# Turning q and k by crossbar DMA transposes instead of on TensorE, in an attention plus feed-forward kernel

## The chip, the cores and the metric

One core of a Trainium2 chip. The time is the device time of one execution, in microseconds (us). Kernels that are compared were run in turn on the same chip. Runs of different sittings are set beside each other too; the kernel before took 235.2 to 236.7 us in all of them. In traces, PE is TensorE, PEld its weight loads, DVE is VectorE, ACT is ScalarE, POOL is GpSimd, SP is SyncE; a "q" after an engine is its queue of DMA issues. SBUF is the memory on the core; PSUM is the one into which TensorE writes.

## The reference, cut to what matters

```python
def _attn_ref(q, k, v, n_global, n_local):      # q, k, v: [4, 8, 768, 64]
    scores = scale * np.matmul(q, k.transpose(0, 1, 3, 2))
    # keep keys that are global (pos < 8) or at most 95 rows back; a bias by distance per head
    ...
    a = np.exp(scores - max); a = a / sum
    return np.matmul(a, v)

def _moe_ref(x, w_in, w_out):                   # x: [3072, 512], w_in: [512, 2048]
    h = np.maximum(x @ w_in, 0.0)
    return h * h @ w_out                        # ... cut
```

The attention output, [3072, 512], is the input of the feed-forward.

## The kernel before: the parts that matter

The 3072 rows are cut into eight half batches of 384 rows (numbered 0 to 7). While TensorE does the feed-forward of one half batch, the attention of the next is strewn among its matmuls. Two matmul layers take most of the time: "hps" (layer 1, 64 matmuls of 384 columns for each half batch) and "yps" (layer 2, 48 matmuls of 512 columns).

Scores need q and k with the head dimension on the partitions. The kernel before turns them on TensorE, and an engine that is free copies the result out of PSUM:

```python
def turn(x, a):                         # one pair of heads of half batch x
    def emit(e):
        state["ps"] = trp = ps_att.tile([P, 2, HT, P], FP16, name="trp", tag="att")
        for i, st in enumerate((x.sq, x.sk)):
            for t in range(HT):         # 2 x 3 transposes of 128x128
                nc.tensor.transpose(out=trp[:, i, t, :], in_=st[:, t, 2 * a:2 * a + 2, :],
                                    identity=ident)
    job = plan.pe(6 * 0.056, emit, x.q_in + x.k_in + [ident_op], [att])
    ...                                 # evac: PSUM to bt.qk, on ACT or DVE
    # fix_k: DVE copies parts of the turned k to bt.kb, the keys of the tile before
    x.qk_ops[a] = ops + [plan.add(costs, fix_k, [ops[1]])]
```

Two things decide the order of instructions. TensorE's own order is a list written by hand (`merge` puts attention jobs between feed-forward jobs). The order on DVE, ACT, POOL and SP comes from a planner that runs once, at build time: it gives each operation a cost and a time of landing, and always emits the one that could start first.

```python
class Plan:
    def load(self, dur, emit, needs=(), rank=None):
        op = Op({"POOL": 0.9}, emit, needs, rank, 1.0, land=dur)   # lag 1.0
    def run(self):
        while self.rest or any(self.queues.values()):
            ...                          # earliest possible start wins; ties go by rank
            op.done = end + op.lag       # when a later operation may count on it
            op.emit(e)                   # this fixes its place in the engine's queue
```

What the planner believes about time does not delay anything on the chip; there, semaphores do. But it decides which instruction stands in front of which, and each engine's queue keeps that order.

```python
y_p = ctx.enter_context(tc.tile_pool(name="yp", bufs=3))          # output rows
...
def evac(e):                             # in layer2
    y = y_p.tile([P, d_model], FP32, name="y", tag="y")
    copy(e, y, st["ps"])
    nc.sync.dma_start(out=out[r0:r0 + P, :], in_=y)               # SP's queue
```

q, k and v are loaded by POOL with a cast from float32 to float16, nine loads for each half batch.

The softmax here doesn't subtract the row's maximum and nothing guards it: scores larger than these inputs give would overflow.

Of the kernel before, what the change touches and what calls it, by code (L numbers as in the profile page):

```python
# [8 lines left out]
FP32 = mybir.dt.float32  # L9
# [4 lines left out]
P = 128  # L14
# [125 lines left out]
def kernel(  # L140
# [11 lines left out]
    nc = tc.nc  # L152
# [3 lines left out]
    d_model, d_ff = moe_w_in.shape  # L156
    NT = S // P
    NPAIR = H // 2
    NFT = d_ff // P
    NCT = d_model // P  # L160
    HALF = S // 2
    HT = HALF // P
    NHB = 2 * B
    GR = 32
# [16 lines left out]
    plan = Plan(1.0, 24.0)  # L181
# [5 lines left out]
    def copy(e, out, in_):  # L187
        if e == "ACT":
            nc.scalar.copy(out=out, in_=in_)  # L189
        else:  # L190
            eng(e).tensor_copy(out=out, in_=in_)  # L191
# [75 lines left out]
    def list_loads(x):  # L267
        r0 = x.half * HALF
        prev = halves[x.hb - 2] if x.hb >= 2 else None
        before = [prev.turned[-1]] if prev else []  # L270
        vbefore = [halves[x.hb - x.half - 3].attended[-1]] if x.hb >= 4 else []

        def rows(src, name, t):
            def emit(e):
                if getattr(x, name, None) is None and name != "v":
                    setattr(x, name, stage_p.tile([P, HT, H, D], FP16, name=name, tag=name))
                dst = (x.bt.v[:, x.half * HT + t, :, 0:D] if name == "v"
                       else getattr(x, name)[:, t, :, :])
                nc.gpsimd.dma_start(out=dst, in_=src[x.b, :, r0 + t * P:r0 + (t + 1) * P, :]  # L279
                                    .rearrange("h p d -> p h d"))  # L280
            return plan.load(0.62, emit, vbefore if name == "v" else before)

        if x.half == 0:
            def start(e):
                new_batch(x.bt)
                nc.vector.memset(x.bt.v[:, :, :, D:D + 1], 1.0)
            x.bt.op = plan.add({"DVE": 0.1}, start, vbefore, rank=0)
        if x.hb:
            x.q_in = [rows(q, "sq", t) for t in range(HT)]
            x.k_in = [rows(k, "sk", t) for t in range(HT)]  # L290
            x.v_in = [rows(v, "v", t) for t in range(HT)]
        else:
            raw = {n: stage_p.tile([P, HT, H, D], FP32, name=n, tag=n, bufs=1)
                   for n in ("rq", "rk")}
            x.q_in, x.k_in, x.v_in = [], [], []

            def fetch(name, src, t, eng, e, lag):
                op = plan.add({e: 0.5}, lambda e: eng.dma_start(
                    out=raw[name][:, t], in_=src[0, :, t * P:(t + 1) * P, :].rearrange(
                        "h p d -> p h d")), rank=-1)  # L300
                op.lag = lag
                return op

            def cast(dst, name, t, f):
                def emit(e):
                    if getattr(x, dst, None) is None:
                        setattr(x, dst, stage_p.tile([P, HT, H, D], FP16, name=dst, tag=dst))
                    copy(e, getattr(x, dst)[:, t], raw[name][:, t])
                return plan.add({"DVE": 0.42, "ACT": 0.54}, emit, [f], rank=0)
            k0 = fetch("rk", k, 0, nc.scalar, "ACT", 3.5)  # L310
            q0 = fetch("rq", q, 0, nc.sync, "SP", 3.5)
            x.q_in.append(cast("sq", "rq", 0, q0))
            x.k_in.append(cast("sk", "rk", 0, k0))
            for t in range(HT):
                if t:
                    x.q_in.append(rows(q, "sq", t))
                    x.k_in.append(cast("sk", "rk", t, fetch("rk", k, t, nc.sync, "SP", 4.0 + t)))
                if t < 2:
                    x.v_in.append(rows(v, "v", t))
            x.v_in.append(rows(v, "v", 2))  # L320
        for l in x.v_in:
            l.needs.append(x.bt.op)
# [15 lines left out]
    def tiles_before(x):  # L338
        return (1, HT - 1) if x.half == 0 else (HT - 1, NT - 1)

    def fix_v(x):
# [9 lines left out]
        costs = {"POOL": 0.6 + 2.1 * n} if x.hb > 1 else {"DVE": 0.2 + 0.65 * n}  # L351
        x.vb_op = plan.add(costs, emit, x.v_in)

    def turn(x, a):
        state = {}

        def emit(e):
            state["ps"] = trp = ps_att.tile([P, 2, HT, P], FP16, name="trp", tag="att")
            warm(trp.rearrange("p i t c -> p (i t c)"))
            for i, st in enumerate((x.sq, x.sk)):  # L360
                for t in range(HT):
# [4 lines that stand above are left out]
        def evac(i):  # L366
            def emit(e):
                copy(e, x.bt.qk[:, i, a, x.half * HALF:(x.half + 1) * HALF],
                     state["ps"][:, i].rearrange("p t c -> p (t c)"))
            return plan.after(job, {"ACT": 0.39, "DVE": 0.31}, emit)  # L370
        ops = [evac(0), evac(1)]
        t0, t1 = tiles_before(x)

        def fix_k(e):
            kt = x.bt.qk[:, 1, a, :].rearrange("p (t c) -> p t c", c=P)
            copy(e, x.bt.kb[:, a, t0 - 1:t1 - 1, GR:P], kt[:, t0:t1, GR:P])
            copy(e, x.bt.kb[:, a, t0 - 1:t1 - 1, 0:GR],
                 kt[:, 0:1, 0:GR].to_broadcast([P, t1 - t0, GR]))
        n = t1 - t0
        costs = {"DVE": 0.2 + 0.08 * n}  # L380
        if x.hb == 0:
            costs["POOL"] = 0.5 + 0.17 * n
        x.turned.append(job)
        x.qk_ops[a] = ops + [plan.add(costs, fix_k, [ops[1]])]

    GROUPS = {
        0: ([(0, 0), (1, 0), (1, 1)], [(2, 0), (2, 1)]),
# [161 lines left out]
    def layer2(x, j, m0):  # L549
        st = x.l2.setdefault(j, {})  # L550

        def emit(e):
            if m0 == 0:
                st["ps"] = ps_big.tile([P, 512], FP32, name="yps", tag="big")
            for m in range(m0, m0 + 4):
                nc.tensor.matmul(st["ps"], lhsT=x.h2[:, m, j * P:(j + 1) * P],  # L556
                                 rhs=w_out_sb[:, m, :], start=m == 0, stop=m == NFT - 1)
        job = plan.pe(4 * 0.216, emit, 
                      [x.h2_ops[max(c for c in x.h2_ops if c <= j * P)][m]
                       for m in range(m0, m0 + 4)] + [w_out_op[m0 // 4]], [big] if m0 == 0 else [])  # L560
        if m0 == 0:
            st["users"] = job.users
        else:
            job.users = st["users"]
            job.users[0].append(job)
        if m0 + 4 == NFT:
            def evac(e):
                y = y_p.tile([P, d_model], FP32, name="y", tag="y")
                copy(e, y, st["ps"])
                r0 = x.hb * HALF + j * P  # L570
                nc.sync.dma_start(out=out[r0:r0 + P, :], in_=y)
            plan.after(job, {"ACT": 0.52, "DVE": 0.63}, evac)

    for x in halves:
        x.turned, x.attended = [], []
# [97 lines left out]
    def tile_to_x(x, t, a0):  # L673
# [13 lines left out]
        for a in (a0, a0 + 1):  # L687
            x.x_ops[a, t] = op

    def attention(x):  # L690
        jobs = [lambda: fix_v(x)]
        for a in range(NPAIR + 3):
            if a < NPAIR:
                jobs.append(lambda a=a: turn(x, a))
            if 0 <= a - 1 < NPAIR:
                jobs.append(lambda a=a - 1: score(x, a))
            if 0 <= a - 2 < NPAIR:
                jobs.append(lambda a=a - 2: attend(x, a))
            if 0 <= a - 3 < NPAIR:
                jobs.append(lambda a=a - 3: to_x(x, a))  # L700
        return jobs

    def merge(main, side, start, stop):
        done = 0
        for i, f in enumerate(main):
            if i >= start:
                want = len(side) if i >= stop else (i - start) * len(side) // (stop - start)
                while done < want:
                    side[done]()
                    done += 1  # L710
            f()
        for f in side[done:]:
            f()

    def l1(x, m0=0):
        return [lambda m=m: layer1(x, [m]) for m in range(m0, NFT)]

    def l2(x):
        return [lambda j=j, m0=m0: layer2(x, j, m0) for j in range(HT) for m0 in range(0, NFT, 4)]
# [38 lines left out]
    for hb in range(1, NHB):  # L758
        x = halves[hb]
        if hb + 1 < NHB:  # L760
            list_loads(halves[hb + 1])
        main = l2(x0)[6:] + l2(x) if hb == 1 else l1(x) + l2(x)
        side = attention(halves[hb + 1]) if hb + 1 < NHB else []
        merge(main, side, 1, len(main) - 3)
    with tc.manual_schedule():
        order = plan.run()

# [34 lines left out]
```

## Time and profile before

The kernel before takes 235.71 us (median of 4 runs, 235.53 to 236.65). The page of its profile says, in this order: the span; busy time of each engine; busy tenths in 40 slices of the span, with the granted TensorE clock (the share of full speed at which the chip let TensorE run) in tenths and the DMA engines' share; the chain of waits that ended last; and two groups of DMA issues with the median time from issue to landing as their last number.

```profile
span 233.5 us, 5024 instructions
PE 221.1 (95%) x2023; PEld 133.8 (57%) x2023; DVE 126.0 (54%) x340; ACT 139.1 (60%) x319; POOL 86.2 (37%) x100
...
PE   7675999999999999999999999999999999999993
...
PEclk9999799999999999999999999999999999999999
DMA  8999999999159907951099107941002100111012
...
PE 88%; POOL 5%; DMA 4%; DVE 0%; issue 0%; ACT 0%; POOLq 0%
...
out_dram<-y SPq DMA_DIRECT2D x24, 256.0 KB, 2.0
...
sq<-in_q_dram POOLq DMA_DIRECT2D x23, 128.0 KB, 5.8
```

TensorE is busy for 90% or more of every slice from the fifth to the last but one, and the chain of waits is 88% TensorE. The waits of the other engines cost nothing there. The DMA row is full for the first ten slices (weights and first loads) and then comes and goes.

| | TensorE in one half batch, steady state |
|---|---|
| layer 1, layer 2 | 64 x 0.1625 + 48 x 0.216 = 20.8 us |
| scores, values, output turns | 4 x 0.45 + 4 x 0.34 + 4 x 0.17 = 3.8 us |
| q and k turns | 4 x 0.33 = 1.3 us |
| measured, start of layer 1 to the next start | 25.95 and 26.4 us in turn |

The turn is read from the timeline of TensorE (start, length, engine and line, what, how many):

```profile
106.62 0.33 PE L362 MATMUL trp<-ident,sq 128*128 128x128 f16 x3
106.78 0.33 PE L362 MATMUL trp<-ident,sk 128*128 128x128 f16 x3
106.95 1.46 PE L508 MATMUL hps<-xt,w_in_sb 128*128 128x384 f16 x8
```

From the first transpose to the next layer 1 matmul are 106.95 - 106.62 = 0.33 us for six transposes, 55 ns each. The length of the record (0.33 us for three) overlaps with the next; the spacing is what a turn costs. The Trainium skill, "TensorE: Matmul & The Clock Gate", Part 4, gives about 275 ns for one transpose in a kernel; in a row, this trace has 55 ns from start to start.

### The profile page before, as it was taken

What the parts mean: (1) busy time and instruction counts of PE and PEld (TensorE: products, weight loads), DVE (VectorE), ACT (ScalarE), POOL (GpSimd) and SP (SyncE); (2) the same over time, 40 slices, a digit from 0 to 9 for tenths busy, and PEclk for the clock granted to TensorE, in tenths of its full rate; (3) what the DMA queues carried; (4) which work ended last, traced back from release to release, by engine and by line L of the source; (5) the groups of instructions that cost most, each with busy time, mean ns of one, the idle gap of its engine ahead of it and who ended that gap; (6) DMA issues with size and microseconds to landing.
All of it is one profiled execution on the core that took longest, in us unless ns stands there. A gap on an engine that the chain in (4) does not pass through costs nothing.

```text
span 233.5 us, 5024 instructions
## 1 busy us (share of the span) xinstructions
PE 221.1 (95%) x2023; PEld 133.8 (57%) x2023; DVE 126.0 (54%) x340; ACT 139.1 (60%) x319; POOL 86.2 (37%) x100
## 2 busy tenths in 40 slices
PE   7675999999999999999999999999999999999993
PEld 6553689654555566556655565556655565556541
DVE  5395799441376279425864279325863279323300
ACT  4693797671564598328961598328961598327521
POOL 8948723894457307670292107560000000000000
PEclk9999799999999999999999999999999999999999
DMA  8999999999159907951099107941002100111012
GB/s 149 168 194 155 200 206 193 156 149 108 45 77 164 148 0 50 162 87 46 0 120 171 49 3 51 162 82 45 3 1 93 45 4 0 48 45 45 0 48 90
DMA packets 82583, 20.77 MB, mean 89 GB/s; under 512 B 75392, under 2 KB 79488, under 8 KB 82560
## 3 DMA queue, kind: packets, MB, share of 16 engines
q0 software_dynamic: 74944, 13.11, 74.5%
q1 hardware_dynamic: 6576, 7.08, 9.1%
q10 hardware_dynamic: 1040, 0.26, 0.5%
q8 instruction: 16, 0.26, 0.5%
q14 instruction: 7, 0.06, 0.1%
HBM read 27.26 MB, written 6.29 MB: 144 GB/s over the span
## 4 chain that ended last, share of the span: by engine, by line
PE 88%; POOL 5%; DMA 4%; DVE 0%; issue 0%; ACT 0%; POOLq 0%
PE hps L508 37%; PE yps L556 36%; PE sp L409 5%; PE trp L362 4%; DMA sk<-in_k_dram 4%; PE av L464 4%; PE trx L488 2%; POOL sq L279 2%; POOL v L279 1%; POOL sk L279 1%; POOL w_in_sb L327 1%; ACT y L189 0%; DVE ident L226 0%; DVE qk L191 0%; POOL dist L220 0%
## 5 line engine op out<-in xcount | busy, mean ns | idle before, releaser
L508 PE MATMUL hps<-xt,w_in_sb 128*128 128x384 f16 (+2 forms) x576 | 93.8, 311 | 0.2 <-DMA w_in_sb<-in_moe_w_in_dram 0.2
L556 PE MATMUL yps<-w_out_sb,h 128*128 128x512 f16 x384 | 91.9, 379 | 0.0
L508 PEld LDWEIGHTS <-w_in_sb 128*128 128x128 f16 x576 | 51.4, 99 | 27.7 <-DMA w_in_sb<-in_moe_w_in_dram 0.4
L532 ACT ACTIVATE hr<-hps 128x384 f16<-128x384 f32 (+1 forms) x109 | 56.3, 517 | 12.0 <-PE hps L508 9.8
L543 DVE TENSOR_TENSOR h<-hr 128x768 f16<-128x768 f16 (+1 forms) x68 | 36.8, 541 | 38.0 <-ACT hr L532 36.9
L556 PEld LDWEIGHTS <-h 128*128 128x128 f16 x384 | 34.5, 98 | 33.6
L424 ACT ACTIVATE ex<-sp 128x384 f16<-128x384 f32 x112 | 44.4, 510 | 4.2 <-PE sp L409 4.1
L189 ACT COPY y<-yps 128x512 f32<-128x512 f32 x22 | 12.9, 585 | 55.1 <-PE yps L556 55.1
L279 POOL DMA_DIRECT2D sq<-in_q_dram x23 | 20.8, 914 | 38.0 <-PE trp L362 36.5
L189 ACT COPY qk<-trp 128x384 f16<-128x384 f16 (+1 forms) x43 | 19.9, 506 | 11.4 <-DVE qk L191 10.4
L191 POOL COPY vb<-v 32x520 f16<-32x520 f16 (+3 forms) x18 | 19.3, 1070 | 19.1 <-DMA v<-in_v_dram 18.5
L279 POOL DMA_DIRECT2D v<-in_v_dram x24 | 21.4, 918 | 7.3 <-DMA w_out_sb<-in_moe_w_out_dram 3.3
L279 POOL DMA_DIRECT2D sk<-in_k_dram x21 | 18.6, 908 | 5.9 <-DMA w_out_sb<-in_moe_w_out_dram 3.1
L440 DVE TENSOR_TENSOR phat<-ex,mask 128x768 f16<-128x768 f16 x32 | 16.4, 553 | 5.4 <-ACT ex L424 5.1
L191 DVE COPY qk<-trp 128x384 f16<-128x384 f16 (+1 forms) x19 | 6.9, 365 | 17.5 <-PE trp L362 13.4
L473 DVE TENSOR_TENSOR tm<-av,rec 128x384 f16<-128x384 f32 x28 | 15.6, 557 | 1.0
L464 PEld LDWEIGHTS <-phat 128*128 128x128 f16 x312 | 13.2, 98 | 4.8
L464 PE MATMUL av<-v,phat 128*128 128x65 f16 x192 | 13.2, 193 | 0.0
L436 DVE TENSOR_TENSOR phat<-ex,mask 128x768 f16<-128x768 f16 (+1 forms) x24 | 10.7, 486 | 3.6 <-ACT ex L424 3.5
L464 PE MATMUL av<-vb,phat 128*128 128x65 f16 x120 | 12.1, 193 | 0.0
L191 DVE COPY kb<-qk 128x96 f16<-128x96 f16 (+4 forms) x58 | 10.2, 222 | 3.5 <-ACT qk L189 2.0
L362 PE MATMUL trp<-ident,sk 128*128 128x128 f16 x84 | 10.0, 226 | 1.5 <-DMA sk<-in_k_dram 1.5
(59 smaller groups left out, 154.8 us busy)
## 6 DMA issues: line engine op xcount, KB each, us to landing
out_dram<-y SPq DMA_DIRECT2D x24, 256.0 KB, 2.0
v<-in_v_dram POOLq DMA_DIRECT2D x24, 128.0 KB, 6.3
sq<-in_q_dram POOLq DMA_DIRECT2D x23, 128.0 KB, 5.8
sk<-in_k_dram POOLq DMA_DIRECT2D x21, 128.0 KB, 5.9
w_in_sb<-in_moe_w_in_dram POOLq DMA_DIRECT2D x4, 512.0 KB, 9.0
w_out_sb<-in_moe_w_out_dram POOLq DMA_DIRECT2D x4, 512.0 KB, 14.3
rk<-in_k_dram SPq DMA_DIRECT2D x2, 256.0 KB, 6.2
rk<-in_k_dram ACTq DMA_DIRECT2D x1, 256.0 KB, 4.6
```

What stands on the lines that cost most here:

```text
L189: nc.scalar.copy(out=out, in_=in_)
L191: eng(e).tensor_copy(out=out, in_=in_)
L279: nc.gpsimd.dma_start(out=dst, in_=src[x.b, :, r0 + t * P:r0 + (t + 1) * P, :] .rearrange("h p d -> p h d"))
L362: nc.tensor.transpose(out=trp[:, i, t, :], in_=st[:, t, 2 * a:2 * a + 2, :], identity=ident)
L424: nc.scalar.activation(out=st["ex", g][:, h, 0:n], in_=st[g][h][:, 0:n], func=AF.Exp, scale=scale)
L440: eng(e).tensor_tensor(out=phat[:, :, c0:c0 + n].rearrange("p e (i c) -> p e i c", c=P), in0=ex[:, :, 0:n].rearrange("p e (i c) -> p e i c ...
L464: nc.tensor.matmul(av[:, h, j, :], lhsT=phat[:, h, c * P:(c + 1) * P], rhs=rhs, start=n == 0, stop=n == len(mine) - 1)
L473: nc.vector.tensor_tensor(out=st["tm"].rearrange("p t e d -> p e t d"), in0=av[:, :, :, 0:D], in1=rec[:, :, :, None].to_broadcast([P, 2, H ...
L508: nc.tensor.matmul(st["ps"][:, i * n:(i + 1) * n], lhsT=w_in_sb[:, kk, m * P:(m + 1) * P], rhs=x.xt[:, kk, c0:c1], start=kk == 0, stop=kk ...
L532: nc.scalar.activation(out=o, in_=i, func=AF.Relu)
L543: eng(e).tensor_tensor(out=x.h2[:, m0:m0 + width, c0:c1], in0=hr, in1=hr, op=ALU.mult)
L556: nc.tensor.matmul(st["ps"], lhsT=x.h2[:, m, j * P:(j + 1) * P], rhs=w_out_sb[:, m, :], start=m == 0, stop=m == NFT - 1)
```

## The change

The turns of half batches 2 to 7 go from TensorE to the DMA engines. Six crossbar transposes (DMAs that transpose on their way) of 128 KB for each half batch, issued from SP's queue, write q and k turned straight into SBUF; no PSUM, no copy out. As TensorE is what bounds the kernel, 24 turns fewer should be 24 turns of time. The freed places are used to spread scores, values and output turns evenly over the feed-forward. Stores of the output become operations of their own in the plan, because they share SP's queue with the transposes.

```diff
-        before = [prev.turned[-1]] if prev else []
+        before = prev.turned if prev else []          # a load waits for these transposes
 ...
+    def turn_by_dma(x):
+        for t in range(HT):
+            for i, (src, loads) in enumerate((("sq", x.q_in), ("sk", x.k_in))):
+                def emit(e, i=i, t=t, name=src):
+                    nc.sync.dma_start_transpose(
+                        out=x.bt.qk[:, i, :, r0 + t * P:r0 + (t + 1) * P],
+                        in_=getattr(x, name)[:, t].rearrange("p h d -> p (h d)"))
+                op = plan.add({"SP": 1.2}, emit, [loads[t], x.bt.op])
+                op.lag = 2.5
+                ops.append(op)
+        x.turned += ops
+        for a in range(NPAIR):
+            x.qk_ops[a] = ops + [plan.add(*fix_k(x, a), ops)]     # kb copies, on DVE
 ...
-                nc.sync.dma_start(out=out[r0:r0 + P, :], in_=y)
+            plan.add({"SP": 0.6}, lambda e: nc.sync.dma_start(out=..., in_=st["y"]), [y_op])
 ...
     def attention(x):
+            jobs.append((0.02 + 0.2 * a, lambda a=a: score(x, a)))
+            jobs.append((0.02 + 0.2 * a + 0.17, lambda a=a: attend(x, a)))
+            jobs.append((0.02 + 0.2 * a + 0.3, lambda a=a: to_x(x, a)))
 ...
+            fix_v(halves[hb + 1])
+            turn_by_dma(halves[hb + 1])
-        merge(main, side, 1, len(main) - 3)
+        merge(main, side)
```

Cut: how `merge` places a job at its fraction of the feed-forward, and the removed TensorE branch.

More of the change, by code (lines that the diff above doesn't have):

```diff
@@ L352, in fix_v, with fix_k, emit @@
         x.vb_op = plan.add(costs, emit, x.v_in)
+    def fix_k(x, a):
+        t0, t1 = tiles_before(x)
+        def emit(e):
+            kt = x.bt.qk[:, 1, a, :].rearrange("p (t c) -> p t c", c=P)
+            copy(e, x.bt.kb[:, a, t0 - 1:t1 - 1, GR:P], kt[:, t0:t1, GR:P])
+            copy(e, x.bt.kb[:, a, t0 - 1:t1 - 1, 0:GR],
+                 kt[:, 0:1, 0:GR].to_broadcast([P, t1 - t0, GR]))
+        return {"DVE": 0.2 + 0.08 * (t1 - t0)}, emit
     def turn(x, a):
@@ L371, in turn @@
         ops = [evac(0), evac(1)]
-        t0, t1 = tiles_before(x)
-        def fix_k(e):
-            kt = x.bt.qk[:, 1, a, :].rearrange("p (t c) -> p t c", c=P)
-            copy(e, x.bt.kb[:, a, t0 - 1:t1 - 1, GR:P], kt[:, t0:t1, GR:P])
-            copy(e, x.bt.kb[:, a, t0 - 1:t1 - 1, 0:GR],
-                 kt[:, 0:1, 0:GR].to_broadcast([P, t1 - t0, GR]))
-        n = t1 - t0
-        costs = {"DVE": 0.2 + 0.08 * n}
-        if x.hb == 0:
-            costs["POOL"] = 0.5 + 0.17 * n
-        x.turned.append(job)
-        x.qk_ops[a] = ops + [plan.add(costs, fix_k, [ops[1]])]
+        x.turned.append(job)
+        x.qk_ops[a] = ops + [plan.add(*fix_k(x, a), [ops[1]])]
+    def turn_by_dma(x):
+        r0 = x.half * HALF
+        ops = []
+        for t in range(HT):
[10 more added lines that the diff above has]
+            x.qk_ops[a] = ops + [plan.add(*fix_k(x, a), ops)]
     GROUPS = {
@@ L567, in evac @@
             def evac(e):
-                y = y_p.tile([P, d_model], FP32, name="y", tag="y")
-                copy(e, y, st["ps"])
-                r0 = x.hb * HALF + j * P
-                nc.sync.dma_start(out=out[r0:r0 + P, :], in_=y)
-            plan.after(job, {"ACT": 0.52, "DVE": 0.63}, evac)
+                st["y"] = y_p.tile([P, d_model], FP32, name="y", tag="y")
+                copy(e, st["y"], st["ps"])
+            r0 = x.hb * HALF + j * P
+            y_op = plan.after(job, {"ACT": 0.52, "DVE": 0.63}, evac)
+            plan.add({"SP": 0.6}, lambda e: nc.sync.dma_start(out=out[r0:r0 + P, :], in_=st["y"]),
+                     [y_op])
     for x in halves:
@@ L690, in attention, with merge @@
     def attention(x):
-        jobs = [lambda: fix_v(x)]
-        for a in range(NPAIR + 3):
-            if a < NPAIR:
-                jobs.append(lambda a=a: turn(x, a))
-            if 0 <= a - 1 < NPAIR:
-                jobs.append(lambda a=a - 1: score(x, a))
-            if 0 <= a - 2 < NPAIR:
-                jobs.append(lambda a=a - 2: attend(x, a))
-            if 0 <= a - 3 < NPAIR:
-                jobs.append(lambda a=a - 3: to_x(x, a))
-        return jobs
-    def merge(main, side, start, stop):
-        done = 0
-        for i, f in enumerate(main):
-            if i >= start:
-                want = len(side) if i >= stop else (i - start) * len(side) // (stop - start)
-                while done < want:
-                    side[done]()
-                    done += 1
-            f()
-        for f in side[done:]:
-            f()
+        jobs = []
+        for a in range(NPAIR):
+            jobs.append((0.02 + 0.2 * a, lambda a=a: score(x, a)))
+            jobs.append((0.02 + 0.2 * a + 0.17, lambda a=a: attend(x, a)))
+            jobs.append((0.02 + 0.2 * a + 0.3, lambda a=a: to_x(x, a)))
+        return sorted(jobs, key=lambda j: j[0])
+    def merge(main, side):
+        for i, f in enumerate(main):
+            while side and side[0][0] * len(main) <= i:
+                side.pop(0)[1]()
+            f()
+        for _, g in side:
+            g()
     def l1(x, m0=0):
```

## The prediction

> **What bounds the kernel now.** TensorE. The busy table gives PE 95% of 233.5 us (221.1 us), ACT 60%, DVE 54%, POOL 37%. In the table by stretches PE is 20.00 of 20 us busy from 50 us to 210 us, and the chain of waits is 88% PE. The waits list gives PE only about 9 us of waits, all in the opening. So from about 52 us on the time is a sum of PE work. The timeline of PE shows one half batch in 25.95 us (104.02 to 129.97) or 26.42 us (77.60 to 104.02): feed-forward 64 x 0.1625 + 48 x 0.216 = 20.8 us, scores about 4 x 0.45, values 4 x 0.34, output turns 4 x 0.17, and the q/k turns 4 x 0.33 us (106.62 to 106.95 is one turn: six transposes 55 ns apart, though each record lasts 0.22 us).
>
> **What the change does.**
> - Removes from PE 24 turns (144 transposes) of half batches 2 to 7: 24 x 0.33 = 7.9 us, all on the critical path. Removes 48 PSUM-to-SBUF copies, 35 on ACT (0.50 us), 13 on DVE (0.36 us): shorter queues, no direct gain.
> - Adds 36 crossbar transposes of 128 KB on SP's queue, six per half batch, in 26 us. The Trainium skill ("Advanced Engine Details and Errata", X-Bar Transpose) calls them as fast as regular DMAs, 350-400 GB/s; that would be (estimate) 0.35 us of data each. No trace here shows one yet. With issue and completion (a plain 256 KB store lands in 2.0 us) I expect 1 to 2 us of queue each and 2 to 3 us to landing: under half the queue's time.
> - Moves scores and values. PE has less work between a score and its values: for pair 1, 16 layer-1 matmuls and a turn, 2.8 us plus the score's own 0.44. In half batches of odd number the trace shows exponentials 0.6 us after the score's start, 1.65 us long, then two mask products of 1.0 us: about 3.4 us. So I expect a small new PE wait, up to 0.5 us, there.
> - kb copies now wait for DMA and stand in DVE's in-order queue before mask products. If loads (about 4 us from last issue to landing) plus transposes are late, DVE blocks and PE follows. I work out half batch 5 as the tightest: its last k lands near 81.5 us, transposed near 84 us, and DVE gets there near 82.5 us; the mask product needs it only about 84.3 us. About 1 us of PE wait; half batches 4, 6 and 7 have a microsecond or so of room.
> - y stores stand behind transposes on SP; three y buffers cover about 10 us, enough.
>
> **Sum.** 235.6 - 7.9 + about 1.8 of new waits = 229.5 us. Opening and tail unchanged.
>
> **What would show it.** PE busy falls by about 8 us or a little more in busy time of records; a steady half batch takes 24.7 to 25.2 us; no turn of lines with "trp" after 32 us; transposes land in under 3 us; ACT busy falls by about 17 us; the waits list has PE values behind DVE mask products of under 3 us in all; DVE kb waiting for DMA of 1 to 4 us.
>
> **What would make it wrong.** Transposes that take over 3 us of queue each: kb late, DVE blocked, PE waiting several us per half batch, up to a loss. Less likely, y stores stuck behind them and PSUM held. On the good side, no new waits at all: 227.5 us.
>
> Faster by over 2% (under 230.9) 0.62, within 2% 0.31, slower 0.07.

## The result, and the profile after

The changed kernel takes 252.95 us (median of 4 runs, 251.23 to 253.35). The ratio to the kernel before is 1.0709, with a 95% interval of 1.0651 to 1.0766: 7% slower. Here and below a ratio is the mean time of one kernel's runs over that of the other's of the same rounds, so it is not quite the ratio of the medians quoted. Executions over 1.5% slower than the fastest of the same kernel are left out of the means.

```profile
span 250.9 us, 4778 instructions
PE 220.0 (88%) x1879; PEld 127.6 (51%) x1879; DVE 124.6 (50%) x322; ACT 127.2 (51%) x289; POOL 86.2 (34%) x100
...
PE   6764999997099498899997499999999999999994
...
PEclk9999799999779889999999779999999999999999
DMA  9999999999999999908999411002100210021012
...
PE 48%; DMA 35%; DVE 6%; POOL 5%; SPq 3%; issue 2%; ACT 0%; POOLq 0%; DVEq 0%
...
out_dram<-y SPq DMA_DIRECT2D x24, 256.0 KB, 2.0
...
sq<-in_q_dram POOLq DMA_DIRECT2D x23, 128.0 KB, 10.4
...
qk<-sq SPq DMA_TRANSPOSE x18, 7.2
```

TensorE's row now has holes in the slices from the tenth to the twenty-third, its share falls from 95% to 88%, and the granted clock dips to 0.7 or 0.8 beside the holes. The chain of waits is no longer TensorE's: 35% of it is DMA. The DMA row stays full up to the seventeenth slice. A transpose lands 7.2 us after its issue; the planner counted on 2.5 us. Loads of q land after 10.4 us instead of 5.8.

Where in time the loss arises shows in the start of layer 1 of each half batch, read from the timelines (us):

| | layer 2 begins | hb 2 | hb 3 | hb 4 | hb 5 | hb 6 | hb 7 | end |
|---|---|---|---|---|---|---|---|---|
| before | 51.67 | 77.60 | 104.02 | 129.97 | 156.39 | 182.34 | 208.75 | 233.5 |
| after | 51.87 | 91.07 | 118.44 | 151.14 | 176.50 | 201.12 | 226.48 | 250.9 |
| difference | 0.2 | 13.5 | 14.4 | 21.2 | 20.1 | 18.8 | 17.7 | 17.4 |

There are two kernels in one here. From 151 us on a half batch takes 25.36 or 24.61 us, 1.1 to 1.3 us less than before: the 0.33 us of each of the four turns are really gone. Before that, 21 us are lost. The list of waits (engine, line, what it waited for: us in all, times, longest) names the place:

```profile
DVE kb L191 <- DMA qk<-sk: 25.2, 4, 8.9
...
PE av L480 <- DVE phat L452: 11.3, 2, 7.9
...
PE trx L504 <- DVE tm L489: 5.1, 1, 5.1
...
PE av L480 <- DVE phat L456: 1.8, 3, 0.9
```

DVE stood for 25.2 us at copies to "kb" that wait for a transpose of k, four times. TensorE then waited 11.3 + 5.1 + 1.8 = 18.2 us for DVE. The timeline of DVE shows three of the four (the idle time before an instruction, and what ended it, in brackets):

```profile
66.30 2.36 DVE L191 COPY kb<-qk 128x288 f16<-128x288 f16 x6 [8.91 <-DMA qk<-sk]
68.58 0.87 DVE L452 TENSOR_TENSOR phat<-ex,mask 128x768 f16<-128x768 f16 x2
...
85.52 0.37 DVE L191 COPY kb<-qk 128x96 f16<-128x96 f16 x2 [5.60 <-DMA qk<-sk]
...
85.97 0.89 DVE L452 TENSOR_TENSOR phat<-ex,mask 128x768 f16<-128x768 f16 x2
...
139.63 1.28 DVE L191 COPY kb<-qk 128x288 f16<-128x288 f16 x2 [7.09 <-DMA qk<-sk]
140.84 0.17 DVE L487 RECIPROCAL rec<-av 128x6 f32<-128x6 f32 x1
```

DVE idled 8.9 us before the kb copies of half batch 3, 5.6 us before those of half batch 4 and 7.1 us before those of half batch 7. What stands behind them in the queue is of quite another half batch. At 139.63 us DVE waits for keys of half batch 7, whose scores TensorE computes from 201 us on; the reciprocal behind it, at 140.84 us, belongs to half batch 4 and is what TensorE needs now. The instruction listing of the built program shows the same order:

```
194 L559 TensorTensor h_1761<-hr 128x768 [waits Activation_49]
195 L191 TensorCopy kb<-qk 128x3x96 [waits DMAHW7_49,DMAHW6_49,DMAHW2_49]
196 L191 TensorCopy kb<-qk 128x3x32
197 L487 Reciprocal rec<-av 128x6 [waits PE_49]
```

TensorE's own timeline answers at the same moments:

```profile
69.17 0.57 PE L480 MATMUL av<-v,phat 128*128 128x65 f16 x4 [7.91 <-DVE phat L452]
...
70.65 2.70 PE L572 MATMUL yps<-w_out_sb,h 128*128 128x512 f16 x8
...
73.36 1.89 PE L572 MATMUL yps<-w_out_sb,h 128*128 128x512 f16 x8
...
86.57 0.57 PE L480 MATMUL av<-v,phat 128*128 128x65 f16 x4 [3.36 <-DVE phat L452]
```

It waited 7.9 us for the mask product at 68.58 us and 3.4 us for the one at 85.97 us. After the first wait eight layer 2 matmuls take 2.70 us; the next eight take 1.89 us. After this wait the granted clock was 0.62 (69.2 to 73.3 us), then 1.00 again (73.36 to 75.2 us); after the other two long waits it was 0.74 (86.6 to 92.0 us) and 0.50 (141.7 to 147.0 us).

The sum: between 51.87 and 151.14 us the changed kernel took 99.3 us, the one before 78.3 us, so 21.0 us more, although 12 turns (12 x 0.33 = 4.0 us) were gone. That makes 25 us of new loss, of which 18.2 us are the waits for DVE. The other 7 us fit the lower clock (0.83 from 57 to 77 us, 0.93 from 77 to 151 us): TensorE was busy for 81.1 of the 99.3 us at a mean clock of 0.91, and 0.91 x 81.1 = 73.8 us, while the kernel before without its 12 turns needs 78.3 - 4.0 = 74.3 us at full clock. No experiment separates the lower clock from the waits that come with it.

### The profile page after: what moved, and what is told of

Its sections match the earlier page's. It is cut to its first block, busy times and chain, and to the rows that moved or that the text cites. A ratio compares the mean times of both kernels' runs of the same rounds, so it can differ in the third digit from the quotient of the medians.

```text
span 250.9 us, 4778 instructions
## 1 busy us (share of the span) xinstructions
PE 220.0 (88%) x1879; PEld 127.6 (51%) x1879; DVE 124.6 (50%) x322; ACT 127.2 (51%) x289; POOL 86.2 (34%) x100
## 4 chain that ended last, share of the span: by engine, by line
PE 48%; DMA 35%; DVE 6%; POOL 5%; SPq 3%; issue 2%; ACT 0%; POOLq 0%; DVEq 0%
PE yps L572 24%; PE hps L524 17%; DMA v<-in_v_dram 15%; DMA w_out_sb<-in_moe_w_out_dram 6%; DMA qk<-sk 5%; DMA w_in_sb<-in_moe_w_in_dram 3%; DMA sk<-in_k_dram 3%; PE av L480 3%; PE sp L425 3%; SPq L392 2%; POOL vb L191 2%; DVE phat L456 2%; DVE h L559 2%; POOL v L279 2%; DMA sq<-in_q_dram 2%
## 5 line engine op out<-in xcount | busy, mean ns | idle before, releaser
L572 PE MATMUL yps<-w_out_sb,h 128*128 128x512 f16 x384 | 94.1, 393 | 0.0
L548 ACT ACTIVATE hr<-hps 128x384 f16<-128x384 f32 (+1 forms) x109 | 55.8, 512 | 20.3 <-PE hps L524 17.7
L572 PEld LDWEIGHTS <-h 128*128 128x128 f16 x384 | 36.5, 101 | 40.3 <-issue 5.3
L440 ACT ACTIVATE ex<-sp 128x384 f16<-128x384 f32 x112 | 43.8, 486 | 25.5 <-PE sp L425 25.5
L559 DVE TENSOR_TENSOR h<-hr 128x768 f16<-128x768 f16 (+1 forms) x68 | 38.0, 560 | 20.3 <-ACT hr L548 19.6
L191 DVE COPY kb<-qk 128x96 f16<-128x96 f16 (+4 forms) x58 | 12.9, 323 | 25.8 <-DMA qk<-sk 25.2
L480 PE MATMUL av<-v,phat 128*128 128x65 f16 x192 | 14.9, 200 | 11.9 <-DVE phat L452 11.3
L480 PEld LDWEIGHTS <-phat 128*128 128x128 f16 x312 | 13.6, 101 | 20.2 <-DVE phat L452 12.4
L456 DVE TENSOR_TENSOR phat<-ex,mask 128x768 f16<-128x768 f16 x32 | 17.7, 593 | 5.1 <-ACT ex L440 5.1
L550 DVE TENSOR_SCALAR hr<-hps 128x384 f16<-128x384 f32 x15 | 8.3, 556 | 17.8 <-PE hps L524 17.3
L191 DVE COPY xt<-trx 128x384 f16<-128x384 f16 (+1 forms) x18 | 6.2, 351 | 16.6 <-PE trx L504 16.6
L504 PE MATMUL trx<-ident,tm 128*128 128x128 f16 x84 | 9.3, 223 | 5.1 <-DVE tm L489 5.1
L487 DVE RECIPROCAL rec<-av 128x6 f32<-128x6 f32 x28 | 5.5, 197 | 14.6 <-PE av L480 13.7
## 6 DMA issues: line engine op xcount, KB each, us to landing
sq<-in_q_dram POOLq DMA_DIRECT2D x23, 128.0 KB, 10.4
```

The lines of the kernel that those rows point to most:

```text
L191: eng(e).tensor_copy(out=out, in_=in_)
L440: nc.scalar.activation(out=st["ex", g][:, h, 0:n], in_=st[g][h][:, 0:n], func=AF.Exp, scale=scale)
L456: eng(e).tensor_tensor(out=phat[:, :, c0:c0 + n].rearrange("p e (i c) -> p e i c", c=P), in0=ex[:, :, 0:n].rearrange("p e (i c) -> p e i c ...
L480: nc.tensor.matmul(av[:, h, j, :], lhsT=phat[:, h, c * P:(c + 1) * P], rhs=rhs, start=n == 0, stop=n == len(mine) - 1)
L504: nc.tensor.transpose(out=st["trx"][:, t, :], in_=st["tm"][:, t, :, :], identity=ident)
L548: nc.scalar.activation(out=o, in_=i, func=AF.Relu)
```

## The experiments

The theories:

- **A, placement.** The data come early enough. The planner put the kb copies where it believed a transpose has landed. DVE keeps that order, so it stands at a copy that nobody needs yet.
- **B, supply.** Loads and transposes together cannot bring q and k in time, wherever the copies stand.
- **C, order.** The even spread of scores and values on TensorE is what stalls.

And for the long landing: the crossbar itself is slow, or transposes queue behind each other, or the DMA engines are shared with the loads.

### 1. kb copies placed late

```diff
-            x.qk_ops[a] = ops + [plan.add(*fix_k(x, a), ops)]
+            x.qk_ops[a] = ops + [plan.add(*fix_k(x, a),
+                                          ops + [halves[x.hb - 1].attended[min(a + 2, 3)]])]
```

> One edit to the changed kernel: each kb copy of a half batch may be placed in DVE's order only after the values of pair a+2 (at most 3) of the half batch before it, so far later than the planner puts it, and still before the score that reads it. Transposes, loads and the order on TensorE stay. Theory A (the data are early enough; the loss is DVE's in-order queue standing at kb copies placed where the planner believed a transpose lands 2.5 us after issue, while it lands after 7.2 us): DVE's wait for DMA falls from 25.2 us to under 5 us, time 227 to 232 us. Theory B (transposes and loads together cannot deliver q and k in time for the scores): the wait moves to the scores and the time stays above 245 us. Theory C (the new order of scores and values on TensorE is itself what stalls): PE still waits for DVE mask products over 10 us in all, time above 240 us.

Measured: 233.99 us (232.06 to 235.18, ratio 0.9911, 0.9857 to 0.9966), so 19 us less than the changed kernel by one line of plan. The transposes landed no sooner (median 7.4 us for those of q). Three lines of the list of waits:

```profile
ACT y L189 <- DMA out_dram<-y: 5.0, 2, 4.0
...
PE hps L524 <- ACT y L189: 3.2, 1, 3.2
...
DVE kb L191 <- DMA qk<-sk: 2.2, 1, 2.2
```

DVE's wait for transposes fell from 25.2 to 2.2 us. B and C fall as the main cause. The time is still 2 us above what A expected, and the list says why: ACT, about to copy a result y out of PSUM, waited 5.0 us for the store of an earlier y to free its buffer, and TensorE 3.2 us behind it. Those stores stand in SP's queue among transposes that wait for their loads. The longest of these waits, from the timelines of SP and ACT:

```profile
65.07 0.58 ACT L189 COPY y<-yps 128x512 f32<-128x512 f32 x1 [0.52 <-PE yps L572]
...
72.78 2.58 SPq L392 DMA_TRANSPOSE qk<-sq  x2
75.45 0.53 SPq L588 DMA_DIRECT2D out_dram<-y  x1
...
81.59 0.58 ACT L189 COPY y<-yps 128x512 f32<-128x512 f32 x1 [3.99 <-DMA out_dram<-y]
```

The row copied by 65.65 us was stored only from 75.45 us on, behind two transposes whose loads had come late (the first load at 72.76 us), and its buffer came free 6.0 us after that.

### 2. The planner's landing time of a transpose corrected

```diff
-                op.lag = 2.5
+                op.lag = 8.0
```

> One number of the changed kernel: the planner's landing time of a transpose, 2.5 becomes 8.0 us. Theory A (a wrong constant made the planner place kb copies too early): most of the loss comes back, 229 to 238 us, DVE's wait for transposes under 10 us. If the loads' landing time, which the planner also takes too short, is as much to blame as the transposes': half batch 7's wait (7.1 us in the changed kernel) stays and the time is 238 to 246 us. Theory B or C: above 245 us.

Measured: 246.13 us (243.04 to 246.47, ratio 1.0405). DVE's wait for transposes fell to 16.3 us only. The expectation of A failed in its size: the right landing time for the transposes alone does not mend the plan. The second expectation comes near (238 to 246 us), but what was to stay, the wait for half batch 7, fell from 7.1 to 3.0 us, and half batch 5 now waited 5.9 us.

### 3. Late kb copies, and the order of before on TensorE

```diff
-        merge(main, side)                     # even spread
+        merge(main, side, 1, len(main) - 3)   # as before, without its turns
```

> As e1_kb_late (late kb copies, transposes by DMA), but scores, values and output turns stand among the feed-forward as in the kernel before, without its q/k turns. Theory A says that the order matters little: within 2 us of e1. Theory C says that this is where the time went: more than 5 us below e1. If the even spread was needed once the turns were gone: 1 to 4 us above e1.

Measured: 236.10 us (235.61 to 237.20, ratio 1.0024), 2.1 us above the run of late kb copies with the spread. Taken alone this would say that the spread is worth 2 us. But here ACT waited 8.3 us for y stores, in the run with the spread 5.0 us; the comparison is clouded and was made again below (run 8).

### 4. Plain copies in place of the transposes

```diff
-                    nc.sync.dma_start_transpose(out=..., in_=...)
+                    nc.sync.dma_start(out=..., in_=...)      # same bytes, same place; wrong values
```

> The changed kernel with each crossbar transpose replaced by a plain SBUF-to-SBUF DMA copy of the same 128 KB from the same queue at the same place; the result is wrong on purpose. If the crossbar itself is slow: the copies land in 2 to 3.5 us and the time falls below 240 us. If it is the 16 DMA engines, shared with the loads, that make anything land late: the copies land in 5 to 8 us too and the time stays at 244 to 254 us.

Measured in one look: 247.54 us. The group of issues (least, median and longest issue in ns) and the time to landing (least, median, longest us), first of the changed kernel, then of this one:

```profile
L392 SPq DMA_TRANSPOSE qk<-sq x18: 1188/1227/2296, 41.8 to 129.4; - x18
...
DMA to landing us min/median/max: 2.5/7.2/9.4
```

```profile
L392 SPq DMA_DIRECT2D qk<-sq x18: 593/594/690, 42.2 to 124.9; - x18
...
DMA to landing us min/median/max: 2.3/6.5/8.9
```

A plain copy of the same bytes landed after 6.5 us in the median, a transpose after 7.2 us, and DVE still waited 18.8 us. So the crossbar is not what makes the landing long. The time is 5.4 us below the changed kernel's median; this is one look, and whether the shorter issue makes the difference is not shown. A transpose does cost SP twice the issue (1.23 against 0.59 us). A warning came with this run: its result still passed the comparison with the reference, though q and k were not turned. The reference draws q and k with a spread of 0.1, so the scores have a spread of about 0.01 (an estimate: 0.125 x 0.01 x the root of 64) and hardly move the output. Passing says little about q and k, here and in the other runs.

### 5. Five y buffers on top of run 1

```diff
-    y_p = ctx.enter_context(tc.tile_pool(name="yp", bufs=3))
+    y_p = ctx.enter_context(tc.tile_pool(name="yp", bufs=5))
```

> e1_kb_late with five buffers for the output rows y instead of three. In e1 ScalarE waited 5.0 us for the store of an earlier y, which stood behind transposes in SP's queue, and TensorE waited 3.2 us behind that. If that is what e1 still loses: those waits fall under 1 us and the time falls by 2 to 4 us against e1, to 229 to 232 us. If it only moves to another wait: within 1 us of e1.

Measured: 229.46 us (median of three fast runs, 229.33 to 231.72; one run of 234.27 us counted as slow), ratio 0.9757 (0.9697 to 0.9818). No wait for a y store is left in the list. As expected, the time fell against run 1, by 3.6 us (the means: 233.8 and 230.2 us).

### 6 and 7. Loads held back until the transposes of the half batch before have landed

```diff
+            def gate(e):                      # POOL reads the transposed tiles before it loads on
+                nc.gpsimd.tensor_copy(out=seen_sb, in_=...)   # 6 columns of qk
+            before = before + [plan.add({"POOL": 0.2}, gate, last.turned)]
```

Run 6 has it on top of run 5, run 7 on top of the changed kernel alone.

> e5_y5 with a small copy on POOL that reads the transposed q and k of a half batch before the loads of the next one are issued, so that loads and transposes overlap less on the 16 DMA engines. Contention theory: transposes land in a median of 3 to 5 us instead of 7.4, loads of q in 6 to 7 us instead of 10; the time is within 2 us of e5 since no engine waits on them there. If landing times stay above 6.5 us with few loads in flight, contention with loads is not their cause.

> The changed kernel with that gate alone: kb copies again where the planner puts them with its landing time of 2.5 us. Contention theory: transposes land in 3 to 5 us, nearer to what the planner assumed, DVE's wait for them falls from 25.2 us to 8 to 16 us and the time to 238 to 246 us. If placement matters whatever the landing time (each load and transpose chain now starts later): 246 us or more.

Measured: run 6 took 230.95 us (230.13 to 233.06, ratio 0.9798), as run 5. Its transposes landed after 6.8 us in the median (least 3.4, longest 10.4), not 3 to 5. Loads of q landed after 4.4 us instead of about 10, better than expected. Run 7, one look, took 245.03 us, in the range expected, but with transposes landing after 6.5 us and DVE waiting 19.4 us for them, which is more than the 8 to 16 us expected. Counted from the trace, a mean of 4.9 loads was in flight beside a transpose in run 5 and 2.8 in run 6. So the expectation was wrong, and by its own words the loads were not the cause. But the gate took away less than it seems: at the moment when a transpose was issued, 4.1 loads were in flight in run 6 and 5.2 in run 5. Whether loads are the cause had to be asked more sharply: run 9.

### 8. Run 5 with the order of before on TensorE

The edit is that of run 3 on top of run 5.

> e5_y5 with scores, values and output turns where the kernel before has them. It separates the spread from the rest with both other waits mended. My prediction holds that the spread brings nothing by itself (it costs up to 0.5 us per odd half batch): within 1.5 us of e5. If the spread is worth its place: 2 us or more above e5.

Measured: 229.50 us (229.45 to 230.68), ratio 0.9741 (0.9705 to 0.9776): faster than the kernel before, and the best. Against run 5 (0.9757) there is no difference. The spread brings nothing once the y stores are out of the way, so what run 3 showed was those. In the steady state a half batch takes 24.61 and 25.22 us here, 24.61 and 25.36 us with the spread. The page of this run:

```profile
span 227.5 us, 4777 instructions
PE 213.7 (94%) x1879; PEld 125.6 (55%) x1879; DVE 125.7 (55%) x327; ACT 125.3 (55%) x284; POOL 86.6 (38%) x100
...
PE   6576899999979999999999999999999999999993
...
PEclk9988799999999999999999999999999999999999
DMA  7999999999999999999999900111001100111012
```

TensorE's holes are gone from its row but for one slice of 0.7 (two waits of 1.6 us in all for DVE's mask products), while the DMA row is as full as in the changed kernel, for longer. What DMA carries was not the problem; who waited for it was.

### 9. Transposes with no load beside them

On top of run 6, POOL touches the staged q and k in place after all nine loads have landed, and the transposes wait for that.

```diff
+        def touch(e):
+            for s in (x.sq, x.sk):
+                nc.gpsimd.tensor_copy(out=s[:, :, 0, 0:2], in_=s[:, :, 0, 0:2])
+        touched = plan.add({"POOL": 0.4}, touch, [x.vb_op] + x.q_in + x.k_in)
```

> e6_gate, and in addition a tiny in-place copy on POOL keeps the transposes of a half batch back until all nine loads of it have landed, so that no load is in flight beside them. It measures the transposes' own landing time. Contention with loads: six transposes issued 1.2 us apart land in 2.3 to 3.5 us each. If the transposes themselves, queued behind each other, make the 7 us: they still land in 5 us or more. Time not predicted closely (the chain load, transpose, load becomes serial): 230 to 245 us.

Measured in one look (249.26 us, more than the loose guess: in this serial chain TensorE waits 14.9 us for transposes directly). The landing of all 36 (least, median, longest us):

```profile
DMA to landing us min/median/max: 2.4/2.4/4.5
```

2.4 us in the median, although the six of a half batch were still issued 1.3 to 2.6 us apart, mostly with one other still in flight and never more than two. So neither the transpose nor other transposes make the 7 us. The loads do. The changed kernel's own trace agrees, without any gate: of its 36 transposes, the three that were issued with no load in flight landed after 2.5, 2.6 and 3.6 us; the five with four loads after 6.0 us in the median; the 14 with six to eight after 7.0 us or more, but for one of 6.3 us. The planner's 2.5 us is the landing time of a transpose on an idle DMA; in the kernel it is three times that. The Trainium skill, "DMA: Bandwidth & Descriptors", section "Issuing engines are not separate DMA queues", says that DMAs of all engines run on the same 16 DMA engines and interleave; these numbers agree.

### 10. Both landing times of the planner near the measured ones

```diff
+            if x.hb > 1:
+                op.lag = 7.0      # loads; was 1.0
-                op.lag = 2.5
+                op.lag = 8.0      # transposes
```

> The changed kernel with both of the planner's landing times set near the measured ones: transposes 8.0 us (as in e2_lag8), and 7.0 instead of 1.0 us of lag for the loads of half batches 2 to 7. e2 got back only part; the theory is that its DVE waits (16.3 us) remained because the planner still believed the loads early. Then DVE's wait for transposes falls under 6 us and the time to 231 to 238 us. If the waits stay above 12 us and the time above 242 us, a planner with right landing times does not help and only decoupling the copies does.

Measured: 235.97 us (235.42 to 238.60, ratio 1.0035). The time is in the range expected and 10 us under run 2, so the planner's belief about loads was as much to blame as that about transposes. DVE's wait fell to 10.1 us, not under 6. A better guess helps; taking the copies off the guess (runs 1, 5 and 8) helps more.

### 11. y stores from ACT's queue

The edit is on top of run 3, with three y buffers: the store is issued by `nc.scalar` in place of `nc.sync`.

> e3_kb_late_old_order with three y buffers, as in the changed kernel, but the y stores issued from ScalarE's queue instead of SP's. If y stores waited because they stood behind transposes in SP's queue: ScalarE's wait for y stores (8.3 us in e3) falls under 1.5 us and the time to 228.5 to 231.5 us, as with five buffers. If the stores were slow because the DMA engines are shared: the wait stays above 4 us and the time above 233 us.

Measured: 249.88 us (249.28 to 250.86, ratio 1.0602), 14 us worse than run 3. Both expectations missed. The list of waits:

```profile
PE sp L425 <- ACT ex L440: 12.6, 1, 12.6
ACT ex L440 <- DMA qk<-sq: 12.4, 1, 12.4
ACT y L189 <- DMA qk<-sq: 11.6, 1, 11.6
```

ACT itself stood 12.4 and 11.6 us, waiting for a transpose of q, with exponentials behind it. A y store has no data from a transpose. The instruction listing shows the link: each DMA issued from SP or ACT waits for one of eight completion semaphores (DMAHW0 to 7), which go round in the order of the plan, so it waits for the DMA eight before it, whichever of the two queues that is on. In the first y stores that is a transpose which itself waits for loads: they went out at 67.32 and 80.31 us, just after the transposes before them on the same semaphore had landed, at 67.25 and 80.23 us. So the store brought its wait along, to an engine that cannot afford it. That y stores in SP's queue were held up by transposes is seen in run 1 and mended by buffers in run 5. This run does not separate the order of the queue from the shared semaphores, but the trace of run 1 does for the long wait there: the semaphore of that store had been free since 66.2 us, so it was the order of the queue (9.8 us from copy to store) and the late landing (6.0 us).

### 12. Five y buffers in the changed kernel, and nothing else

> The changed kernel with five y buffers instead of three and nothing else. Its own trace shows no wait of ScalarE for a y store, so y buffers should be worth nothing as long as DVE stands at the kb copies: 249 to 254 us, DVE's wait for transposes 20 us or more. If the y buffers were an independent loss that adds to the other: 246 to 249.5 us.

Measured in one look: 252.52 us, DVE waiting 25.5 us. The y buffers are worth nothing as long as DVE stands; the second wait only shows once the first is gone.

## Why the prediction was wrong, point by point

It gave 229.5 us and 0.07 for slower; measured were 252.95 us.

The step that failed is the term of new waits in its sum, "about 1.8 of new waits", with "about 1 us" of it for kb copies that block DVE. The runs showed about 25 us in its place: 18.2 us in which TensorE waited for DVE, and about 7 us that fit a lower clock. The mechanism was named; its size rested on landing times that were too short (next points). Run 1 shows that late landing alone is cheap: the transposes landed as late (those of q after 7.4 us), only the copies stood elsewhere, and 19 us came back.

- **What bounds the kernel, and what is removed: right.** TensorE bounded it, and 24 turns of 0.33 us were on its path. The steady half batch was put at 24.7 to 25.2 us; it takes 24.6 and 25.4 us. TensorE's busy time was to fall by about 8 us; at the lower clock it fell only from 221.1 to 220.0 us, in run 8 to 213.7 us. That run 8 takes 229.5 us, the very sum predicted, is luck: it has other places for the kb copies, five y buffers and no spread.
- **"1 to 2 us of queue each and 2 to 3 us to landing": the first holds, the second does not.** The issue takes 1.2 us. The landing takes 7.2 us beside loads and 2.4 us alone (run 9). The estimate came from a plain store that lands in 2.0 us, and I did not ask what else is on the DMA engines when a transpose goes out, although the loads in the same trace landed after 5.8 us. Even the plain stores did not all land in 2.0 us, which is a median of 24: the three that the kernel before issued between 64 and 75 us, beside loads, landed after 4.1, 4.2 and 5.2 us.
- **"Loads (about 4 us from last issue to landing)": too short as well.** Loads of q landed after 10.4 us in the changed kernel. Run 10 against run 2 shows that this counts: 10 us.
- **"I work out half batch 5 as the tightest ... About 1 us of PE wait": right mechanism, wrong size.** DVE blocked in its queue at kb copies was foreseen, but as 1 us. It was 25.2 us on DVE and 18.2 us on TensorE, at half batches 3, 4 and 7 above all. Half batch 3 was not looked at; half batch 7, given room of a microsecond or so, cost 7.1 us of DVE time for data needed 60 us later. I saw that the planner places copies just when it believes them ready, and took that as a small slack: I did not reckon that, where it believes too early, DVE stands (8.9 us at the longest).
- **"Transposes that take over 3 us of queue each: kb late, DVE blocked": the consequence came, not its condition.** The queue was not the trouble; the time to land was.
- **"Three y buffers cover about 10 us, enough": wrong.** It did not show in the changed kernel, where DVE waited first, but cost 3.6 us once that was gone (run 1 against run 5).
- **A "small new PE wait, up to 0.5 us" from the spread in odd half batches: about right.** In the steady state half batches with the spread take 0.14 us more there (25.36 against 25.22 us), and no wait of TensorE over 0.15 us is left. Earlier, in the feed-forward of half batch 2, it waited three times for that mask product, 1.8 us in all, 0.9 us at the longest.
- **ACT busy down by about 17 us:** 139.1 to 127.2 us, 11.9 us. The planner gave ACT copies that DVE had done before (24 in place of 22 copies of y, for one).

## What to carry to other kernels

When an order is fixed ahead of time by believed durations, do not let an in-order engine stand at work that is needed much later: tie such work to an event shortly before its use, and a wrong belief costs little (here one line brought 19 us back, and 2.2 us of DVE's wait stayed). Take the landing time of a DMA from a stretch with the same other traffic, not from an idle one; here the two differ by a factor of three. And when one wait is mended, look at the list of waits again before judging the rest: the y buffers were worth nothing before the first repair and 3.6 us after it, and the spread seemed worth 2 us only while they were short.

## What the Trainium skill lacked or had wrong

- "Advanced Engine Details and Errata", X-Bar Transpose (TRN2), says that transposes are as fast as regular DMAs. For landing this about agrees: 7.2 us against 6.5 us for a plain copy of the same bytes at the same place, both beside loads. That section says nothing of the issue (other pages have sequencer cycles of earlier generations, no measured time): 1.23 us of SP's queue for a transpose of 128 KB, 0.59 us for the plain copy.
- "DMA: Bandwidth & Descriptors", Rules for kernel authors, says that a transpose next to ordinary DMAs needs nothing. For the values, no run here could show it (the output hardly depends on q and k). For the time it lacks that landing went from 2.4 us alone to 7.2 us beside loads, and that it rose with the number of loads in flight (2.5 to 3.6 us with none, 6.0 us with four, in one kernel).
- "TensorE: Matmul & The Clock Gate", Part 4, gives about 275 ns for a 128x128 transpose in a kernel. In a row of six, this trace has 55 ns from start to start; only the record of one is about 220 ns long.
- No page that I read tells that DMAs of SP's and ACT's queues can be tied together by completion semaphores that go round: ACT waited 24.0 us for transposes that it neither issued nor used.
